# Keys with query weights, values with output weights: single loads of 39936-byte rows into four slots

## The chip, the cores and the metric

The kernel runs on one core of one Trainium2 chip. The metric is device time in microseconds (us), median of the runs shown; lower is better. A profile of one execution stands beside it, with times in us from the start of its span.

## The reference

One decode step of a transformer block, batch B=4, one token each, model width D=448, in float32. Attention has 16 query heads on 8 key/value heads of width 256 and looks at the last W=1024 of 4096 cached positions. Behind it stands an MLP with F=1792 hidden units. Cut to what is computed:

```python
def _A_ref(x, k_cache, v_cache, wq, wo):
    q = (x @ wq).reshape(B, 1, 16, 256).transpose(0, 2, 1, 3)
    k = repeat(k_cache[:, :, Sk - W:, :], 2, axis=1)
    v = repeat(v_cache[:, :, Sk - W:, :], 2, axis=1)
    p = softmax(einsum("bhqd,bhkd->bhqk", q, k) * 256 ** -0.5)
    o = einsum("bhqk,bhkd->bhqd", p, v)
    return o.transpose(0, 2, 1, 3).reshape(B, 1, 4096) @ wo

def _B_ref(x, w1, b1, w2, b2):
    return gelu(layernorm(x) @ w1 + b1) @ w2 + b2

h = x + _A_ref(layernorm(x), k_cache, v_cache, wq, wo)
out = h + _B_ref(layernorm(h), w1, b1, w2, b2)
```

Keys and values are 33.6 MB each, all weights together 21.1 MB; each byte is read once.

## The kernel before

The work goes by key/value head g = 0 to 7. `kernel` lays out all arrays on the host so that each load is a block of 128 rows, one for each partition, with its bytes contiguous. All large loads go through one ring of ten slots of 16 KB per partition (L37, L48), all are issued by the SP queue in program order, and each waits there until its slot is free.

For each head there are two loads of keys (`load_k`, L75, 2 MB, rows of 16384 bytes) and two of values (`load_v`, L79). `load_w` (L70) brings the query weights of head g+1 with the output weights of head g in rows of 14336 bytes. The order of the loads is: query weights 0, keys 0, weights, then for each g keys g+1, weights, values g. Head 7's values come in four loads of 1 MB. Then come the output weights of head 7 (wo7), w1 in two loads and w2 in three. The second load of w1 is completed by a small DMA from `w1e` (L53), whose outermost dimension is 8.

TensorE's order is that of the program (L275 to L305). In step g it does:

- `scores(g+1)` (L167): 32 matmuls s (L173), 16 for each half of the keys. VectorE takes the maximum (L177), ScalarE the exponentials (L184).
- `project_q(g+2)` (L152): matmuls pq and pqt.
- `values(g)` (L203): 32 matmuls po (L210) in four groups of eight, c = 0 to 3. After the second group stands `transpose_p(g+1)` (L193), passed in as `between`.
- `output(g)` (L229): VectorE scales po (L231), matmuls pot (L235) turn it, matmuls acc (L245) multiply with the output weights and add up over heads.

For g=7 there is no next head. acc is copied (L295) and folded into ph (L299), `output(7)` adds to ph (L251). `keep_warm` (L270) issues matmuls without use on an idle tile; in `values(7)` two follow each of the first three groups and three the last. Behind it stands the tail: h = x + attention (L336), its two layer norms, the hidden layer pu (L364), Gelu (L378), the transposes put (L383), the second layer py (L395), the sum (L399) and the output DMA (L400).

The four batch rows of a quantity sit on the first four partitions of each quarter of 32 partitions; the tail's matmuls after the first chunk use 4 columns of weights (`m`, L361 and L393). x, transposed, comes in a DMA of its own on the ScalarE queue (L57). x, b2 and b1 for the tail (`rs`) come in four DMAs of four rows (L128).

Of the kernel before, what the change touches and what calls it, by code (L numbers as in the profile page):

```python
# [8 lines left out]
F32 = mybir.dt.float32  # L9
# [18 lines left out]
E8 = 384  # L28
SLOT = 4096
EPS = 1e-5  # L30
SCALE = DH ** -0.5

@with_exitstack
def block_kernel(ctx: ExitStack, tc, x, rows, wq0, ww, kc, vc, wo7, w1, w1e, w2, out):
# [12 lines left out]

    def load(src, cols, name, eighths=0):  # L48
        t = ring.tile([P, SLOT], F32, tag="t", name=name)[:, :cols]
        n = cols - eighths  # L50
        nc.sync.dma_start(t[:, :n], src[:, :n])
        if eighths:
            nc.sync.dma_start(t[:, n:], w1e.rearrange("e (p c) -> e p c", c=E8)[:, :16, :])  # L53
        return t

    xT = const.tile([P, ND, B], F32, name="xT")
    nc.scalar.dma_start(xT, x.rearrange("p (a b) -> p a b", a=ND))  # L57


    def wq_parts(t):  # L60
        parts = [(a, a, slice(0, 512), t[:, a * 512 : (a + 1) * 512]) for a in range(3)]
        for i in range(2):
            parts.append((3, 3 + i, slice(i * 2 * P, (i + 1) * 2 * P), t[:, 3 * 512 :]))
        return parts

    def wo_rows(t):
        return t.rearrange("p (j e) -> p j e", j=4)


    def load_w(g):  # L70
        t = load(ww[g], 8 * D, f"ww{g}")
        return wq_parts(t[:, : 4 * D]), wo_rows(t[:, 4 * D :])


    def load_k(g):  # L75
        return [load(kc[g, i], 2 * B * 512, f"k{g}_{i}").rearrange("p (c b k) -> p c b k", c=2, b=B) for i in range(2)]


    def load_v(g):  # L79
        v, n = [], 2 if g == HKV - 1 else 4  # L80
        for c0 in range(0, NKC, n):
            t = load(vc[g, :, c0 * B * DH : (c0 + n) * B * DH], n * B * DH, f"v{g}_{c0}")
            t = t.rearrange("p (c b d) -> p c b d", c=n, b=B)
            v += [t[:, c : c + 2] for c in range(0, n, 2)]
        return v

# [26 lines left out]
    fold = fold.rearrange("p j q -> p (j q)")  # L113
    rows_of = ident.rearrange("p (j q) -> p j q", j=4)[:, :, :B]
    rows_of_pair = ident.rearrange("p (b q) -> p q b", b=B)
# [86 lines left out]

    def values(g, vt, between=None):  # L203
        if g == HKV - 1:
            tail.append(ps_t.tile([P, 2, 512], F32, tag="t", name="tail"))

        po = ps_o.tile([P, 2, DH], F32, tag="o", name=f"po{g}")
        for c in range(NKC // 2):
            for b in range(B):
                nc.tensor.matmul(  # L210
                    po[b * Q : (b + 1) * Q], pT[g % 2][:, c, b, :], vt[c][:, :, b, :],
                    start=(c == 0), stop=(c == NKC // 2 - 1),
                )
# [15 lines left out]
    def output(g, po, rec, wt):  # L229
        o = work.tile([P, 2, DH], F32, tag="o", name=f"o{g}")  # L230
        nc.vector.tensor_scalar_mul(o, po, rec)  # L231
# [10 lines left out]
        nc.vector.tensor_copy(dst[:, :, :, :B], pt)  # L242
# [12 lines left out]

    wqt = wq_parts(load(wq0, 4 * D, "wq0"))
    d = work.tile([P, ND, B], F32, tag="d", name="d_x")
# [7 lines left out]
    nc.vector.tensor_mul(yT[H:, 4, :B], d[H:, 3, :], rx[H:, :])  # L265
    project_q(0, wqt)

    tail = []

    def keep_warm(n):  # L270
        for _ in range(n):
            nc.tensor.matmul(tail[0][:Q, 0, :], idle[:, :Q], idle, start=True, stop=True)  # L272


    kt = load_k(0)  # L275
    wqt, wot = load_w(0)
    p, rec = scores(0, kt)
    project_q(1, wqt)
    transpose_p(0, p)
    for g in range(HKV):  # L280
        if g + 1 < HKV:
            kt = load_k(g + 1)
        if g + 2 < HKV:
            wqt, wo_next = load_w(g + 1)
        vt = load_v(g)
        if g + 1 == HKV:
            wot = wo_rows(load(wo7, 4 * D, "wo7"))
        if g + 1 < HKV:
            p, rec_next = scores(g + 1, kt)
        if g + 2 < HKV:  # L290
            project_q(g + 2, wqt)
        if g + 1 == HKV:

            accs = once.tile([P, D], F32, tag="u", name="accs")
            nc.scalar.copy(accs, acc)  # L295
            last = ps_s.tile([P, 2, 512], F32, tag="s", name="last")
            ph, pu = last[:, 1, :P].rearrange("p (i c) -> p i c", i=2), last[:, 0, :FQ]
            for j in range(4):
                nc.tensor.matmul(ph[j * Q : (j + 1) * Q], sel, columns(accs, j), start=True, stop=False)  # L299
        po = values(g, vt, (lambda: transpose_p(g + 1, p)) if g + 1 < HKV else None)  # L300
        output(g, po, rec, wot)
        if g + 1 < HKV:
            rec = rec_next
            if g + 2 < HKV:
                wot = wo_next  # L305

    w1t = []
    for a in (0, 2):
        n = 2 * F if a == 0 else F + F // 2
        t = load(w1[:, a * F : a * F + n], n, f"w1_{a}", eighths=E8 if a else 0)  # L310
        w1t += [t[:, :F], t[:, F:]]
    w2t = []
    for i, n in enumerate((8, 4, 2)):
        c0 = len(w2t)
        t = load(w2[:, c0 * D : (c0 + n) * D], n * D, f"w2_{i}").rearrange("p (c e) -> p c e", c=n)
        w2t += [t[:, c, :] for c in range(n)]

# [33 lines left out]
    nc.tensor.matmul(pz, z, rows_of, start=True, stop=True)  # L351
    nc.vector.tensor_copy(zT[:, :, :B], pz)
    hb = once.tile([P, P], F32, tag="hb", name="hb")
# [6 lines left out]
    for a in range(ND):  # L360
        m = Q if a == 0 else B  # L361
        for j in range(4):
            rows, w = w1_part(a, j)
            nc.tensor.matmul(  # L364
                pu[j * Q : j * Q + m, :], zT[rows, a, :m], w, start=(a == 0), stop=(a == ND - 1),
            )
# [19 lines left out]
    dst = gT[:, :12, :].rearrange("p (c j) q -> p c j q", c=3)  # L386
    nc.vector.tensor_copy(dst[:, :, :, :B], put[:, :3])
    for i, rows in enumerate((slice(0, H), slice(H, P))):
        nc.vector.tensor_copy(gT[rows, 12:, :B], put[rows, 3].rearrange("p (j i) q -> p j i q", i=2)[:, :, i, :])
    py = ps_o.tile([P, 2, H], F32, tag="o", name="py")  # L390
    for c in range(NFC):
        for j in range(4):
            m, n = (Q, 2) if c == 0 else (B, 2 if j < 3 else 1)  # L393
            w = columns(w2t[c], j) if n == 2 else w2t[c][:, None, 3 * P :]
            nc.tensor.matmul(  # L395
                py[j * Q : j * Q + m, :n, :], gT[:, c, :m], w, start=(c == 0), stop=(c == NFC - 1),
            )
    res = once.tile([P, P], F32, tag="res", name="res")
    nc.vector.tensor_add(res, py.rearrange("p i c -> p (i c)"), hb)  # L399
    nc.sync.dma_start(out, res)  # L400

# [62 lines left out]
```

## Time and profile before

| what | value |
|---|---|
| time, median of 3 runs | 217.79 us (217.52 to 217.93) |
| profiled execution, span | 215.9 us |
| instructions | 2546 |
| TensorE matmuls busy | 147.9 us, 69% |
| bytes read from HBM | 88.26 MB |
| mean granted TensorE clock | 0.842 |

The profile records one execution; its own time is known as the span from the first to the last instruction, 215.9 us, and the time of a run holds some 2 us more around it. Rows of a group read: line, engine, operation, tile written <- tiles read, shape, count | busy us, mean ns of one | idle time of the engine before them and what ended it. Rows of a stretch read: start:end, length, then busy us and count of TensorE matmuls, weight loads, VectorE, ScalarE and GpSimd, then granted clock, DMA share, GB/s. Rows of the timeline and of the chain begin with start and duration.

### The profile page before, as it was taken

The numbers are of one execution on the slowest core, as the hardware profiler recorded it, in microseconds if no ns is written. First come the engines' busy times: TensorE is split into PE (matmuls) and PEld (weight loads), VectorE is DVE, ScalarE is ACT, GpSimd is POOL, SyncE is SP. The second block draws the span as 40 slices with busy tenths as digits, with TensorE's granted clock in tenths as the row PEclk, the third lists the DMA queues.
The fourth block names the chain that finished last, engine by engine and source line by source line (L and its number), as shares of the span: only waits on it lengthen the run. The fifth ranks groups of instructions, "written<-read, shape, count | busy, mean of one in ns | idle before, by whom it ended". The sixth has DMA issues, their size and how long they took to land.

```text
span 215.9 us, 2546 instructions
## 1 busy us (share of the span) xinstructions
PE 147.9 (69%) x1077; PEld 61.0 (28%) x1077; DVE 35.7 (17%) x138; ACT 20.7 (10%) x49; POOL 5.6 (3%) x17
## 2 busy tenths in 40 slices
PE   0478854578469764776568845876477838789994
PEld 0341413131143303231142304231142203235443
DVE  1411311011110111021200131011201020201230
ACT  0210303000210003000210003000300011000310
POOL 6100000000000000000000000000000000000110
PEclk9999998596967888596958787696959796969999
DMA  6999999999999999999999999999999999999991
GB/s 250 422 425 427 428 432 430 420 428 429 427 431 422 431 421 432 425 431 422 431 428 425 429 425 433 428 425 424 435 419 431 434 423 410 419 427 418 350 396 49
DMA packets 7379, 88.49 MB, mean 410 GB/s; under 512 B 952, under 2 KB 1208, under 8 KB 1736
## 3 DMA queue, kind: packets, MB, share of 16 engines
q1 hardware_dynamic: 7192, 88.28, 97.2%
q8 instruction: 8, 0.13, 0.2%
q10 hardware_dynamic: 176, 0.05, 0.1%
q14 instruction: 3, 0.02, 0.0%
HBM read 88.26 MB, written 0.07 MB: 409 GB/s over the span
## 4 chain that ended last, share of the span: by engine, by line
DMA 72%; PE 22%; issue 2%; DVE 2%; ACT 1%; SPq 0%
DMA v<-vc 53%; DMA k<-kc 16%; PE po L210 6%; PE s L173 2%; DMA xT<-x 2%; PE tail L272 2%; PE py L395 2%; PE last L364 2%; PE pot L235 1%; PE pq L155 1%; PE pqt L161 1%; DVE o L231 1%; PE acc L245 1%; ACT qs L157 1%; PE last L251 0%
## 5 line engine op out<-in xcount | busy, mean ns | idle before, releaser
L210 PE MATMUL po<-v,pT 128*32 128x512 f32 x256 | 44.3, 805 | 12.8 <-DMA v<-vc 12.8
L173 PE MATMUL s<-k,qT 128*32 128x512 f32 x256 | 40.4, 761 | 13.6 <-DMA k<-kc 12.4
L184 ACT ACTIVATE p<-s,nm 128x512 f32<-128x512 f32 x16 | 10.8, 683 | 134.6 <-DVE nm L180 134.6
L173 PEld LDWEIGHTS s<-k,qT 128*32 128x32 f32 x256 | 8.5, 124 | 42.2 <-DVE mx L177 22.8
L177 DVE TENSOR_REDUCE mx<-s 128x1 f32<-128x512 f32 x16 | 11.1, 692 | 53.2 <-PE s L173 53.2
L161 PE MATMUL pqt<-sel,qs 128*128 128x4 f32 x64 | 13.9, 340 | 6.0 <-ACT qs L157 6.0
L155 PE MATMUL pq<-ww,yT 128*32 128x512 f32 (+1 forms) x70 | 7.5, 513 | 14.2 <-DMA ww<-ww 14.2
L210 PEld LDWEIGHTS po<-v,pT 128*32 128x32 f32 x256 | 8.8, 130 | 29.1 <-issue 20.4
L161 PEld LDWEIGHTS pqt<-sel,qs 128*128 128x128 f32 x64 | 13.2, 306 | 10.2 <-ACT qs L157 10.2
L235 PE MATMUL pot<-ident,o 128*128 128x8 f32 x64 | 8.5, 259 | 6.4 <-DVE o L231 6.4
L235 PEld LDWEIGHTS pot<-ident,o 128*128 128x128 f32 x64 | 7.7, 191 | 13.2 <-DVE o L231 13.2
L196 PEld LDWEIGHTS ppt<-ident,p 128*128 128x128 f32 x64 | 7.6, 152 | 11.2 <-issue 11.2
L231 DVE TENSOR_SCALAR o<-po,rec 128x512 f32<-128x512 f32 x8 | 6.0, 751 | 22.1 <-PE po L210 22.1
L196 PE MATMUL ppt<-ident,p 128*128 128x128 f32 x64 | 9.4, 294 | 0.0
L155 PEld LDWEIGHTS pq<-ww,yT 128*32 128x32 f32 x70 | 2.9, 108 | 21.6 <-issue 20.1
L200 DVE COPY pT<-ppt 128x32 f32<-128x32 f32 x16 | 2.3, 187 | 38.7 <-PE ppt L196 38.7
L245 PE MATMUL acc<-ww,oT 128*32 128x448 f32 x56 | 6.7, 551 | 1.9 <-DVE oT L242 1.9
L272 PE MATMUL tail<-idle 128*32 128x512 bf16 x25 | 7.5, 402 | 0.0
L157 ACT COPY qs<-pq 128x512 f32<-128x512 f32 x8 | 4.7, 585 | 21.2 <-PE pq L155 21.2
L149 POOL TENSOR_TENSOR r<-ve_r,mhalf 128x1 f32<-128x1 f32 x2 | 1.1, 542 | 195.2 <-DVE ve_r L148 195.2
L165 DVE COPY qT<-pqt 128x16 f32<-128x16 f32 x16 | 2.1, 170 | 23.8 <-PE pqt L161 23.8
L134 PE MATMUL pm_x<-xT,mean 128*128 128x12 f32 x2 | 0.6, 362 | 5.8 <-DMA xT<-x 5.8
(93 smaller groups left out, 55.9 us busy)
## 6 DMA issues: line engine op xcount, KB each, us to landing
k<-kc SPq DMA_DIRECT2D x16, 2048.0 KB, 34.9
v<-vc SPq DMA_DIRECT2D x14, 2048.0 KB, 37.7
ww<-ww SPq DMA_DIRECT2D x7, 1792.0 KB, 18.4
v<-vc SPq DMA_DIRECT2D x4, 1024.0 KB, 36.1
w<-w SPq DMA_DIRECT2D x2, 1792.0 KB, 24.2
w<-w SPq DMA_DIRECT2D x1, 1152.0 KB, 24.8
wq<-wq SPq DMA_DIRECT2D x1, 896.0 KB, 4.7
wo<-wo SPq DMA_DIRECT2D x1, 896.0 KB
```

The costliest lines, as they stand in the source:

```text
L155: nc.tensor.matmul(pq[j * Q : (j + 1) * Q, cols], yT[:, a, :], w, start=True, stop=True)
L157: nc.scalar.copy(qs, pq)
L161: nc.tensor.matmul(pt[:, i, :], qs[:, i * P : (i + 1) * P], sel[:, :B], start=True, stop=True)
L173: nc.tensor.matmul(s[b * Q : (b + 1) * Q, h, :], qT[g % 2][:, c, b, :], kt[h][:, c, b, :], start=(c == 0), stop=(c == 1),)
L177: nc.vector.reduce_max(mx[:, h : h + 1], s[:, h, :], axis=AX.X)
L184: nc.scalar.activation(p[:, h * 512 : (h + 1) * 512], s[:, h, :], AF.Exp, bias=nm, scale=SCALE, accum_out=sums[:, h : h + 1],)
L196: nc.tensor.transpose(pt[:, c, :], p[:, c * P : (c + 1) * P], ident)
L210: nc.tensor.matmul(po[b * Q : (b + 1) * Q], pT[g % 2][:, c, b, :], vt[c][:, :, b, :], start=(c == 0), stop=(c == NKC // 2 - 1),)
L231: nc.vector.tensor_scalar_mul(o, po, rec)
L235: nc.tensor.matmul(pt[:, c], o[:, i, c * P : (c + 1) * P], rows_of_pair[:, i * REP : (i + 1) * REP, :], start=(i == 0), stop=(i == 1),)
L245: nc.tensor.matmul(acc[i * Q : (i + 1) * Q, :], oT[g % 2][:, i, :], wt[:, i, :], start=(g == 0), stop=(g == HKV - 2),)
L272: nc.tensor.matmul(tail[0][:Q, 0, :], idle[:, :Q], idle, start=True, stop=True)
```

## The change

Ring and slots: four slots of 39936 bytes per partition instead of ten of 16384. A head's keys and the next head's query weights become one array `kw` with rows of 39936 bytes, a head's values and output weights one array `vw`; each is one load. Head 7 has no next query weights and loads 32768 bytes of its row. Head 7's values come in two DMAs into one slot, three quarters and one quarter. wo7 and w1 share a slot (three DMAs), w2 has one (three DMAs of 8, 4 and 2 chunks). `w1e` is gone. The first query weights and the transposed x come as one load (`first`).

`transpose_p(g+1)` moves from the middle of `values(g)` to ahead of it. In `values(7)` only the last group is followed by keep-warm matmuls. The batch rows sit on every eighth partition, so that x and the biases (`rows`, 16 rows) come in one DMA, the output is 16 rows instead of 128, and the tail's matmuls use all 32 columns.

```diff
-E8 = 384
-SLOT = 4096
+GAP = Q // B
+KV = 8 * B * DH
+WC = 4 * D
+SLOT = KV + WC
+V7A = 6 * B * DH
+W1C = 3 * F + F // 2
...
-    ring = ctx.enter_context(tc.tile_pool(name="ring", bufs=10))
+    ring = ctx.enter_context(tc.tile_pool(name="ring", bufs=4))
...
+    t0 = const.tile([P, WC + X0], F32, name="first")
+    nc.sync.dma_start(t0, first)
...
     def load_k(g):
-        return [load(kc[g, i], 2 * B * 512, f"k{g}_{i}").rearrange("p (c b k) -> p c b k", c=2, b=B) for i in range(2)]
+        t = load(kw[g] if g < HKV - 1 else kw[g][:, :KV], f"k{g}")
+        k = t[:, :KV].rearrange("p (h c b k) -> p h c b k", h=2, c=2, b=B)
+        return [k[:, h] for h in range(2)], wq_parts(t[:, KV:]) if g < HKV - 1 else None
...
     def load_v(g):
+        t = load(vw[g], f"v{g}")
+        return chunk_pairs(t[:, :KV]), wo_rows(t[:, KV:])
+
+    def load_v7():
+        t = slot("v7")
+        for a, b in ((0, V7A), (V7A, KV)):
+            nc.sync.dma_start(t[:, a:b], v7[:, a:b])
+        return chunk_pairs(t[:, :KV])
...
-    for j in range(4):
-        nc.scalar.dma_start(rs[j * Q : j * Q + B, :], rows[j])
+    nc.scalar.dma_start(rs[::GAP, :], rows)
+    def spread(t):
+        return t[..., ::GAP]
...
-            if c == 1 and between is not None:
-                between()
-            if g == HKV - 1:
-                keep_warm(2 if c < NKC // 2 - 1 else 3)
+            if g == HKV - 1 and c == NKC // 2 - 1:
+                keep_warm(3)
...
         if g + 1 < HKV:
-            kt = load_k(g + 1)
...
+            kt, wqt = load_k(g + 1)
+            vt, wot = load_v(g)
             p, rec_next = scores(g + 1, kt)
-        if g + 2 < HKV:
-            project_q(g + 2, wqt)
+            if g + 2 < HKV:
+                project_q(g + 2, wqt)
+            transpose_p(g + 1, p)
+        else:
+            vt = load_v7()
+            tw = slot("w1")
+            wot = wo_rows(tw[:, :WC])
+            nc.sync.dma_start(tw[:, :WC], wo7)
+            tw1 = tw[:, WC : WC + W1C]
+            for a, n in ((0, 2 * F), (2 * F, W1C - 2 * F)):
+                nc.sync.dma_start(tw1[:, a : a + n], w1[:, a : a + n])
+            tw2 = slot("w2")
+            for c0, n in ((0, 8), (8, 4), (12, 2)):
+                nc.sync.dma_start(tw2[:, c0 * D : (c0 + n) * D], w2[:, c0 * D : (c0 + n) * D])
...
-            m, n = (Q, 2) if c == 0 else (B, 2 if j < 3 else 1)
+            n = 2 if c == 0 or j < 3 else 1
...
-                py[j * Q : j * Q + m, :n, :], gT[:, c, :m], w, start=(c == 0), stop=(c == NFC - 1),
+                py[j * Q : (j + 1) * Q, :n, :], gT[:, c, :], w, start=(c == 0), stop=(c == NFC - 1),
...
-    nc.sync.dma_start(out, res)
+    nc.sync.dma_start(out, res[::GAP, :])
```

More of the change, by code (lines that the diff above doesn't have):

```diff
@@ L27 @@
 Q = 32
-E8 = 384
-SLOT = 4096
+GAP = Q // B
+KV = 8 * B * DH
+WC = 4 * D
+SLOT = KV + WC
+X0 = 64
+V7A = 6 * B * DH
+W1C = 3 * F + F // 2
 EPS = 1e-5
@@ L33, in block_kernel @@
 @with_exitstack
-def block_kernel(ctx: ExitStack, tc, x, rows, wq0, ww, kc, vc, wo7, w1, w1e, w2, out):
+def block_kernel(ctx: ExitStack, tc, rows, first, kw, vw, v7, wo7, w1, w2, out):
     nc = tc.nc
     const = ctx.enter_context(tc.tile_pool(name="const", bufs=1))
-    ring = ctx.enter_context(tc.tile_pool(name="ring", bufs=10))
+    ring = ctx.enter_context(tc.tile_pool(name="ring", bufs=4))
     work = ctx.enter_context(tc.tile_pool(name="work", bufs=2))
@@ L44, in block_kernel, with slot, load @@
     ps_w = ctx.enter_context(tc.tile_pool(name="ps_w", bufs=1, space=PSUM))
[L48 to L53, printed above, removed]
-        return t
-    xT = const.tile([P, ND, B], F32, name="xT")
-    nc.scalar.dma_start(xT, x.rearrange("p (a b) -> p a b", a=ND))
+    def slot(name):
+        return ring.tile([P, SLOT], F32, tag="t", name=name)
+    def load(src, name):
+        n = src.shape[-1]
+        t = slot(name)[:, :n]
+        nc.sync.dma_start(t, src)
+        return t
+    t0 = const.tile([P, WC + X0], F32, name="first")
+    nc.sync.dma_start(t0, first)
+    xT = t0[:, WC : WC + ND * B].rearrange("p (a b) -> p a b", a=ND)
     def wq_parts(t):
@@ L62, in wq_parts @@
         for i in range(2):
-            parts.append((3, 3 + i, slice(i * 2 * P, (i + 1) * 2 * P), t[:, 3 * 512 :]))
+            parts.append((3, 3 + i, slice(i * 2 * P, (i + 1) * 2 * P), t[:, 3 * 512 : 4 * D]))
         return parts
@@ L67, in wo_rows, with chunk_pairs @@
         return t.rearrange("p (j e) -> p j e", j=4)
-    def load_w(g):
-        t = load(ww[g], 8 * D, f"ww{g}")
-        return wq_parts(t[:, : 4 * D]), wo_rows(t[:, 4 * D :])
     def load_k(g):
-        return [load(kc[g, i], 2 * B * 512, f"k{g}_{i}").rearrange("p (c b k) -> p c b k", c=2, b=B) for i in range(2)]
-    def load_v(g):
[L80 to L85, printed above, removed]
+        t = load(kw[g] if g < HKV - 1 else kw[g][:, :KV], f"k{g}")
+        k = t[:, :KV].rearrange("p (h c b k) -> p h c b k", h=2, c=2, b=B)
+        return [k[:, h] for h in range(2)], wq_parts(t[:, KV:]) if g < HKV - 1 else None
+    def chunk_pairs(t):
+        t = t.rearrange("p (c b d) -> p c b d", c=NKC, b=B)
+        return [t[:, c : c + 2] for c in range(0, NKC, 2)]
+    def load_v(g):
+        t = load(vw[g], f"v{g}")
[5 more added lines that the diff above has]
+        return chunk_pairs(t[:, :KV])
     ident = const.tile([P, P], F32, name="ident")
@@ L113, in block_kernel @@
     fold = fold.rearrange("p j q -> p (j q)")
-    rows_of = ident.rearrange("p (j q) -> p j q", j=4)[:, :, :B]
+    rows_of = ident.rearrange("p (j b e) -> p j b e", j=4, b=B)[:, :, :, 0]
     rows_of_pair = ident.rearrange("p (b q) -> p q b", b=B)
@@ L200, in transpose_p, with values @@
             nc.vector.tensor_copy(pT[g % 2][:, :, :, i * REP : (i + 1) * REP], src[:, :, i, :, :REP])
-    def values(g, vt, between=None):
+    def values(g, vt):
         if g == HKV - 1:
@@ L241, in output @@
         dst = oT[g % 2].rearrange("p (r c) q -> p c r q", r=REP)
-        nc.vector.tensor_copy(dst[:, :, :, :B], pt)
+        nc.vector.tensor_copy(spread(dst), pt)
         for i in range(4):
@@ L254, in output @@
                 )
-    wqt = wq_parts(load(wq0, 4 * D, "wq0"))
     d = work.tile([P, ND, B], F32, tag="d", name="d_x")
@@ L265, in block_kernel @@
     nc.vector.tensor_mul(yT[H:, 4, :B], d[H:, 3, :], rx[H:, :])
-    project_q(0, wqt)
+    project_q(0, wq_parts(t0[:, :WC]))
     tail = []
@@ L299, in block_kernel @@
                 nc.tensor.matmul(ph[j * Q : (j + 1) * Q], sel, columns(accs, j), start=True, stop=False)
-        po = values(g, vt, (lambda: transpose_p(g + 1, p)) if g + 1 < HKV else None)
+        po = values(g, vt)
         output(g, po, rec, wot)
@@ L303, in block_kernel @@
             rec = rec_next
[L304 to L316, printed above, removed]
+    w1t = [tw1[:, a * F : (a + 1) * F] for a in range(3)] + [tw1[:, 3 * F :]]
+    w2t = [tw2[:, c * D : (c + 1) * D] for c in range(NFC)]
     def w1_part(a, j):
@@ L351, in block_kernel @@
     nc.tensor.matmul(pz, z, rows_of, start=True, stop=True)
-    nc.vector.tensor_copy(zT[:, :, :B], pz)
+    nc.vector.tensor_copy(spread(zT), pz)
     hb = once.tile([P, P], F32, tag="hb", name="hb")
@@ L360, in block_kernel @@
     for a in range(ND):
-        m = Q if a == 0 else B
         for j in range(4):
@@ L364, in block_kernel @@
             nc.tensor.matmul(
-                pu[j * Q : j * Q + m, :], zT[rows, a, :m], w, start=(a == 0), stop=(a == ND - 1),
+                pu[j * Q : (j + 1) * Q, :], zT[rows, a, :], w, start=(a == 0), stop=(a == ND - 1),
             )
@@ L386, in block_kernel @@
     dst = gT[:, :12, :].rearrange("p (c j) q -> p c j q", c=3)
-    nc.vector.tensor_copy(dst[:, :, :, :B], put[:, :3])
+    nc.vector.tensor_copy(spread(dst), put[:, :3])
     for i, rows in enumerate((slice(0, H), slice(H, P))):
-        nc.vector.tensor_copy(gT[rows, 12:, :B], put[rows, 3].rearrange("p (j i) q -> p j i q", i=2)[:, :, i, :])
+        nc.vector.tensor_copy(spread(gT[rows, 12:, :]), put[rows, 3].rearrange("p (j i) q -> p j i q", i=2)[:, :, i, :])
     py = ps_o.tile([P, 2, H], F32, tag="o", name="py")
@@ L429 @@
     wo = np.asarray(A_wo).reshape(HKV, 4, P, D).transpose(0, 2, 1, 3).reshape(HKV, P, 4 * D)
-    ww = np.concatenate([wq[1:], wo[:-1]], axis=2)
+    first = np.concatenate([wq[0], xT, np.zeros((P, X0 - ND * B), np.float32)], axis=1)
+    kw = np.concatenate([k, np.concatenate([wq[1:], np.zeros((1, P, WC), np.float32)])], axis=2)
+    vw = np.concatenate([v[:-1], wo[:-1]], axis=2)
     w1 = packed(np.asarray(B_w1))
-    w1e = np.concatenate([w1[:, -E8:].reshape(8, 16 * E8), np.zeros((8, E8), np.float32)], axis=1)
     w2 = np.asarray(B_w2).reshape(4, FQ, D)
@@ L447 @@
     rows = np.concatenate([quadrants(xp), quadrants(b2), quadrants(np.asarray(B_b1).reshape(1, F))], axis=2)
+    rows = rows.reshape(4 * B, -1)
     arrays = {
-        "x": xT, "rows": rows, "wq0": wq[0], "ww": ww, "kc": k, "vc": v, "wo7": wo[-1], "w1": w1, "w1e": w1e, "w2": w2,
+        "rows": rows, "first": first, "kw": kw, "vw": vw, "v7": v[-1], "wo7": wo[-1], "w1": w1, "w2": w2,
     }
@@ L456 @@
     ]
-    out = nc.dram_tensor("out", (P, P), F32, kind="ExternalOutput").ap()
+    out = nc.dram_tensor("out", (4 * B, P), F32, kind="ExternalOutput").ap()
     with tile.TileContext(nc) as tc:
@@ L461 @@
     r = run(nc, [arrays], core_ids=[0])
-    got = np.asarray(r.results[0]["out"]).reshape(4, Q, P)[:, :B, :]
+    got = np.asarray(r.results[0]["out"]).reshape(4, B, P)
     return np.ascontiguousarray(got.transpose(1, 0, 2).reshape(B, 1, 4 * P)[:, :, :D])
```

14 lines of the change are left out of this document (3 added, 11 removed).

## The prediction

> **What bounds the kernel now.** I read the first page from the top: busy shares, the slices, the queues.
>
> ```profile
> span 215.9 us, 2546 instructions
> PE 147.9 (69%) x1077; PEld 61.0 (28%) x1077; DVE 35.7 (17%) x138; ACT 20.7 (10%) x49; POOL 5.6 (3%) x17
> DMA  6999999999999999999999999999999999999991
> GB/s 250 422 425 427 428 432 430 420 428 429 427 431 422 431 421 432 425 431 422 431 428 425 429 425 433 428 425 424 435 419 431 434 423 410 419 427 418 350 396 49
> q1 hardware_dynamic: 7192, 88.28, 97.2%
> HBM read 88.26 MB, written 0.07 MB: 409 GB/s over the span
> ```
>
> No compute engine is near its limit, while the DMA engines are busy in every slice but the first and last. All of it is one queue, and its 88.28 MB don't change. So the first question is what rate the engines give, the second what happens after the stream. The chain that ended last, from the landing of the last piece of v6 (g=6), shows the second (columns: start, us, what):
>
> ```profile
> 183.87 0.04 issue
> 183.91 1.97 PE po L210 x16
> 185.91 0.76 DVE o L231
> 189.65 0.42 PE last L299 x8
> 190.07 1.49 PE po L210 x8
> 195.40 1.14 PE po L210 x5
> 196.57 0.76 DVE o L231
> 199.84 0.65 PE tail L272 x3
> 209.56 2.82 PE py L395 x62
> 212.38 0.09 issue
> 212.47 0.66 PE py L395 x4
> 213.16 0.29 DVE res L399
> ```
>
> From 183.87 on there is no DMA piece: TensorE works through the second half of values(6), output(6), values(7), output(7) and the MLP without a break. Yet the stream isn't slack: py stops for 0.09 us at 212.38, just before its last two chunks, and these are what the last load brings. By stages:
>
> ```profile
> 202.00:206.00 4.00, 4.00 (x33) 1.44 (x32) 0.77 (x4) 1.69 (x3) 0.60 (x2) 1.00 1.02 351
> 210.00:214.00 4.00, 3.00 (x104) 2.37 (x94) 0.29 (x1) 0.00 (x0) 0.00 (x0) 1.00 0.23 89
> ```
>
> (The last three columns are granted clock, DMA share, GB/s.) A share of 0.23 of the last 4 us puts the end of the stream near 211; with its landing that is the stop at 212.38. **Two chains end together**: the stream, and TensorE's work counted from the landing of v6. A gain in the stream alone is worth nothing unless TensorE gains as well, and TensorE gains only by an earlier landing of v6 or by less work behind it.
>
> **The change, the stream.** Rows get longer, their bytes stay. What a row costs beside its bytes, the rates show:
>
> ```profile
> 60.00:90.00 30.00, 20.74 (x130) 8.73 (x130) 3.75 (x14) 2.62 (x6) 0.00 (x0) 0.74 1.01 427
> 64.00:76.00 12.00, 10.57 (x72) 3.66 (x72) 1.22 (x4) 0.00 (x0) 0.00 (x0) 0.78 1.00 426
> 150.00:180.00 30.00, 19.30 (x131) 7.11 (x135) 4.82 (x17) 3.48 (x9) 0.00 (x0) 0.83 1.01 428
> 184.00:191.00 7.00, 5.21 (x48) 1.98 (x49) 0.93 (x2) 0.53 (x1) 0.00 (x0) 0.94 1.01 421
> rs<-rows ACTq DMA_DIRECT2D x4, 11.0 KB
> out<-res SPq DMA_DIRECT2D x1, 64.0 KB
> ```
>
> The 30-us stretches move rows of 16384 B (and 14336 B), 426 to 428 GB/s, middle 427; the stretch 184 to 191 moves v7's 8192-byte rows at 421. On 16 engines a 16384-byte row takes 16 x 16384 / 427 = 613.9 ns, an 8192-byte one 16 x 8192 / 421 = 311.3 ns. Two of the short less one of the long is **8.8 ns per row**; with 426 and 422 it is 5.8, with 428 and 420 11.7. No row of 39936 B is in the trace; at the same price it takes 1475 + 9 ns, or 431 GB/s. Nothing excludes that so long a row is slower; that is a rival below.
>
> Ahead of v6's end the kernel loads 38 times 128 rows (wq0, 16 of k, 14 of v, 7 of ww), afterwards 16 times (first, 8 of k, 7 of v). That is 22 x 128 / 16 = 176 rows fewer per engine: 176 x 8.8 ns = 1.55 us (1.0 to 2.1). To the end of the stream it is 24 loads instead of 48, and w1e's 128 rows go too: 200 rows, 1.75 us. The biases came in four DMAs of 4 rows (11.0 KB each); if these sit on 4 of 16 engines, those carry 4 x 2816 B / 26.7 B per ns = 0.4 us more than the others, and every later load lands with them; 16 rows in one DMA spread to 0.1 us each. Between 0 and 0.3 us earlier; I take 0.3. The stretch at 351 GB/s, where w1_2 and w1e are due, may be w1e's doing and would then go; it lies behind v6 and only moves the end of the stream. So **v6 lands 1.85 us earlier, at 182.0**, and the stream ends about 2.05 us earlier.
>
> Does the stream still run without a break with four slots? A load waits for the slot of the load four before it. A 39936-byte load takes 5.11 MB / 427 = 12.0 us, so three loads behind cover 36 us from landing to release. TensorE is busy 147.9 us over some 17 loads, under 9 us each, and even doubled by its waits that is 18. The SP queue, which issues all of them in order, has nothing else to issue; half of the cover is left. x now lands with wq0 as one load of 0.95 MB, in place of 0.9 MB beside it; the first scores then wait for k0 whole, some 1 us later than now, covered by the 12 us until k1 lands. I cost both at nothing.
>
> **The change, TensorE behind v6.** Now v6 comes in two loads, and half of values(6) is done before 183.87. Afterwards it lands whole, and all 32 matmuls stand behind it. Their price depends on the granted clock:
>
> ```profile
> 135.54 3.60 PE L210 MATMUL po<-v,pT 128*32 128x512 f32 x16 [1.09 <-DMA v<-vc]
> 140.45 1.92 PE L210 MATMUL po<-v,pT 128*32 128x512 f32 x16 [0.28 <-DMA v<-vc]
> 179.09 2.88 PE L210 MATMUL po<-v,pT 128*32 128x512 f32 x16 [2.97 <-DMA v<-vc]
> 176.51:179.92 3.41, 0.83 (x8) 0.34 (x12) 1.00 (x5) 1.45 (x4) 0.00 (x0) 1.00 1.01 425
> 179.92:183.34 3.42, 3.42 (x19) 1.72 (x12) 0.00 (x0) 0.00 (x0) 0.00 (x0) 0.50 0.96 402
> 186.75:190.16 3.41, 2.49 (x28) 1.46 (x32) 0.17 (x1) 0.53 (x1) 0.00 (x0) 1.00 1.02 423
> 190.16:193.58 3.42, 3.42 (x18) 0.88 (x11) 0.00 (x0) 0.00 (x0) 0.00 (x0) 0.50 1.03 429
> 197.00:213.20 16.20, 15.39 (x221) 8.79 (x220) 3.96 (x19) 2.77 (x7) 1.08 (x2) 1.00 0.86 330
> ```
>
> Sixteen take 3.6 us at half clock, 1.95 at full. A stretch of 3.4 us with little work (176.51, with the wait of 2.97) is followed by one at half clock, a busy one by full clock. Afterwards k7 lands at 182.0 - 12.0 = 170.0, and TensorE has 32 score matmuls, 3.9 to 7.2 us; then it waits for the softmax:
>
> ```profile
> L184 ACT ACTIVATE p<-s,nm 128x512 f32<-128x512 f32 x16 | 10.8, 683 | 134.6 <-DVE nm L180 134.6
> L177 DVE TENSOR_REDUCE mx<-s 128x1 f32<-128x512 f32 x16 | 11.1, 692 | 53.2 <-PE s L173 53.2
> ```
>
> That is 0.7 + 2 x 0.7 us, and the transposes, which now stand ahead of values, are too small to count as a burst. So for 4 to 8 us before 182.0 there is almost no matmul work, and values(6) starts at half clock, with between 1.5 and 5 us of it left, since full clock comes only after a stretch of 3.4 us that was busy. With 3.2 us: 14 matmuls in it, 18 in 2.2 us, **5.4 us** (3.9 all full, 7.2 all half); values(6) ends at 187.4.
>
> From its end to the start of values(7) nothing changes: 185.88 to 190.07, 4.2 us. So values(7) starts at 191.6; its first three quarters have landed (182.0 + 7.4), the last lands at 191.8 and is needed 3 us later. Today values(7) takes 190.07 to 196.54, 6.5 us, with six keep-warm matmuls inside it that are removed: at 0.22 us (0.65 for three) at full clock and twice that at half, two and four of them, 1.7 us. That leaves 4.8 with the half-clock stretch lying just on its start, the dearest place; 3.9 without it, 5.5 with all of it. I take 4.6, near the row. It ends at **196.2**, against 196.54: of 1.85 us of earlier landing, 0.3 are left, since 3.4 us of matmuls have come behind the landing and only 1.9 went.
>
> The skill speaks against the change here. The Trainium skill, "TensorE: Matmul & The Clock Gate", section "HAM oscillation — how this bites in real kernels", says that a wait longer than its activity window of about 3.4 us halves the clock for the next burst; the stretches above agree (0.5 behind 2.97 us of waiting). The same page, section "What's actually happening", says that this window runs free of the kernel's start, so that its placement cannot be known beforehand; one trace can't show that.
>
> **The change, the rest.** The MLP's matmuls load 32 columns instead of 4, and the transposed copies write every eighth column:
>
> ```profile
> L395 PE MATMUL py<-w,gT 128*4 128x128 f32 x78 | 3.2, 272 | 0.1
> L395 PE MATMUL py<-w,gT 128*32 128x128 f32 x8 | 0.4, 281 | 0.4 <-DVE gT L387 0.4
> ```
>
> 281 against 272 ns for overlapping matmuls: nothing, at worst 9 ns x 28 in a row of one quarter, 0.25 us. The stop of 0.1 us before the last chunks goes, as the stream ends 2 us earlier. The output shrinks from 128 rows of 512 B to 16, seven fewer on each engine: 7 x (19 + 9 ns) = 0.2 us. **Sum: -0.3 - 0.1 - 0.2 = -0.6 us**, a span of 215.3. The profile gives the span alone; the median of the runs is 1.9 us above it (217.52 to 217.93), which I keep: 217.2.
>
> **The rivals.**
> (1) TensorE meets full clock in both bursts: 182.0 + 3.9 + 4.2 + 3.9 = 194.0, 2.5 earlier; then the stream's end decides, 2.05 + 0.2 earlier: 215.5. Against it speaks the idle time before v6.
> (2) Slower: the half clock falls on both bursts, since a whole load leaves TensorE waiting longer in one piece and the keep-warm matmuls are gone. Up to 182.0 + 7.2 + 4.2 + 5.5 = 198.9, 2.4 later less 0.3; with 6.5 and 5.2, near 218.9. It decides once the two bursts take over 10.9 us together (I took 10.0). That is what the page's rule gives when its window falls badly.
> (3) The long rows don't run faster, so that the change does not do what it is built for: v6 at 183.9, then 5.4 + 4.2 + 4.6 ends at 198.1, 1.5 later less 0.2: 219.1. The 8.8 ns speak against it, for it that it rests on 6 GB/s.
> (4) Waits by slot, not by piece: wo7 shares a slot with w1, whose end lands at 182.0 + 8.3 MB / 427 = 201.5, and output(7) would wait for it some 3 us: 220. Against it:
>
> ```profile
> 207.67 0.69 ACT L378 ACTIVATE u<-u 128x256 f32<-128x256 f32 x2 [3.89 <-DVE u L377]
> 208.14 0.84 PE L383 MATMUL put<-ident,u 128*128 128x16 f32 x6
> ```
>
> TensorE reads the first half of u at 208.14 while ScalarE writes the second until 208.36: pieces are waited for one by one.
>
> **How the numbers follow.** My case 0.46 (own range 216.5 to 217.8), (1) 0.15, (2) 0.20, (3) 0.12, (4) 0.04, others 0.03. Within 0.2%, 217.35 to 218.23, is about what a measurement cannot tell from no change: 0.10 of my case, 0.07 of (2) and the others' 0.03 lie there. Faster: 0.36 + 0.15 = 0.51; same 0.20; slower 0.13 + 0.12 + 0.04 = 0.29. The range 215.5 to 219.0 takes in (1), my case, most of (2) and half of (3).
>
> **What would show it.** The stretches of 30 us at 430 to 432 GB/s; at 427 or less (3) holds. The first matmul of values(6) near 182.0 and 32 of them in 5 to 6 us behind it; the clock row of that stretch at 0.5 or a mix. No DMA stop before py's end. values(7) without a wait for its last quarter. What would make me wrong: TensorE waiting for w1 at output(7), a load issued only after the queue ran dry, or another clock in the 16 us after values(7), which I left at 1.00.

## The result, and the profile after

| | before | after |
|---|---|---|
| median of 20 runs each, us | 217.71 | 217.55 |
| ratio, 95% interval | | 0.9994 (0.9971 to 1.0017) |
| profiled execution, span, us | 215.9 | 217.3 |
| instructions | 2546 | 2466 |

No change that can be measured. The forecast was 217.2 us with the likeliest case "a little faster". One thing the medians hide: nineteen of the twenty runs of before lie within 217.5 to 217.9 us, while the changed kernel's go from 216.6 to 220.65. The ratios, here and below, leave out runs over 1.5% above the fastest of the same kernel: of the changed kernel the five from 220.45 to 220.65 us, of swap two at 223.2. With those five its mean is 218.4 us against 217.8, 0.3% longer; none of them was profiled. The profiled execution took 219.05 us; eleven of the twenty are shorter. Its page begins:

```profile
span 217.3 us, 2466 instructions
PE 151.9 (70%) x1071; PEld 57.4 (26%) x1071; DVE 35.7 (16%) x138; ACT 20.2 (9%) x49; POOL 5.6 (3%) x17
DMA  7999999999999999999999999999999999999930
GB/s 293 435 397 471 426 397 466 426 399 463 434 415 441 426 426 441 444 404 449 434 426 429 441 434 419 441 422 426 456 401 451 405 459 404 393 425 417 420 120 5
q1 hardware_dynamic: 3488, 88.25, 94.9%
```

3488 packets instead of 7192, for the same bytes. The last two slices hold 120 and 5 GB/s, where before they held 396 and 49: the stream ends earlier, although the span is longer. The stretches (granted clock, DMA share, GB/s in the last columns) give the rate, and the stretch from 202, which stood at 351:

```profile
60.00:90.00 30.00, 21.03 (x144) 8.22 (x140) 5.35 (x21) 3.87 (x10) 0.00 (x0) 0.75 0.99 427
90.00:120.00 30.00, 23.57 (x138) 7.03 (x138) 3.49 (x12) 1.94 (x5) 0.00 (x0) 0.68 1.01 432
120.00:150.00 30.00, 18.71 (x130) 6.79 (x130) 4.42 (x14) 1.94 (x5) 0.00 (x0) 0.78 1.00 431
150.00:180.00 30.00, 21.67 (x144) 6.97 (x137) 5.38 (x18) 3.38 (x9) 0.00 (x0) 0.77 0.99 427
202.00:206.00 4.00, 4.00 (x29) 1.56 (x28) 0.99 (x5) 2.09 (x5) 0.38 (x1) 1.00 1.00 420
206.00:210.00 4.00, 4.00 (x32) 1.56 (x28) 1.40 (x5) 0.69 (x2) 0.71 (x2) 1.00 0.50 202
```

Two of the four 30-us stretches reach the 431 to 432 GB/s of the forecast, two stand at 427 as before. From 30 to 180 us the changed kernel averages 430 GB/s and the kernel before 427 (the rows stand under short).

And the chain behind the landing of v6:

```profile
182.48 0.14 issue
182.62 6.21 PE po L219 x32
191.00 1.63 PE acc L252 x8
193.23 0.66 PE last L310 x8
193.89 3.90 PE po L219 x32
197.81 0.76 DVE o L238
210.91 3.30 PE py L395 x66
214.23 0.29 DVE res L399
```

v6 lands at 182.48 instead of 183.87, and py runs through without a stop at its last chunks: the stream no longer decides. But values(6) now takes 6.21 us behind the landing instead of 1.97, and what follows up to values(7) takes 5.06 us (188.83 to 193.89) instead of 4.19. values(7) takes 3.90 instead of 6.47. The sum of those, -1.3 + 4.2 + 0.9 - 2.6, is 1.2 us at the end of values(7). From there to the start of res the chain is 0.2 us shorter (16.44 us, before 16.62), and from res to the end of the span 0.3 us longer, at the output's store. That makes the 1.4 us between the spans.

### The profile page after: what moved, and what is told of

The parts are those of the page before. It is cut to its first block, busy times and chain, and to the rows that moved or that the text cites. A ratio compares the mean times of both kernels' runs of the same rounds, so it can differ in the third digit from the quotient of the medians.

```text
span 217.3 us, 2466 instructions
## 1 busy us (share of the span) xinstructions
PE 151.9 (70%) x1071; PEld 57.4 (26%) x1071; DVE 35.7 (16%) x138; ACT 20.2 (9%) x49; POOL 5.6 (3%) x17
## 3 DMA queue, kind: packets, MB, share of 16 engines
q1 hardware_dynamic: 3488, 88.25, 94.9%
## 4 chain that ended last, share of the span: by engine, by line
DMA 70%; PE 25%; DVE 2%; issue 1%; SPq 1%; ACT 0%
DMA v<-vw 70%; PE po L219 13%; PE acc L252 3%; PE pot L242 2%; PE tail L278 2%; DVE o L238 2%; PE last L364 2%; PE py L395 2%; PE last L258 0%; SPq L59 0%; DVE oT L249 0%; PE put L383 0%; PE last L310 0%; PE tail L328 0%; PE pm L328 0%
## 5 line engine op out<-in xcount | busy, mean ns | idle before, releaser
L182 PE MATMUL s<-k,qT 128*32 128x512 f32 x256 | 46.3, 860 | 24.0 <-DMA k<-kw 17.5
L182 PEld LDWEIGHTS s<-k,qT 128*32 128x32 f32 x256 | 8.4, 136 | 60.4 <-DMA k<-kw 20.6
L186 DVE TENSOR_REDUCE mx<-s 128x1 f32<-128x512 f32 x16 | 11.1, 692 | 73.0 <-PE s L182 73.0
L219 PEld LDWEIGHTS po<-v,pT 128*32 128x32 f32 x256 | 10.6, 151 | 39.4 <-issue 32.8
L170 PE MATMUL pqt<-sel,qs 128*128 128x4 f32 x64 | 9.3, 268 | 6.1 <-ACT qs L166 6.1
L170 PEld LDWEIGHTS pqt<-sel,qs 128*128 128x128 f32 x64 | 8.6, 208 | 10.7 <-ACT qs L166 10.7
L252 PE MATMUL acc<-v,oT 128*32 128x448 f32 x56 | 9.6, 764 | 2.0 <-DVE oT L249 2.0
L164 PE MATMUL pq<-k,yT 128*32 128x512 f32 (+1 forms) x70 | 8.1, 554 | 0.0
L164 PEld LDWEIGHTS pq<-k,yT 128*32 128x32 f32 x70 | 3.7, 124 | 7.4 <-issue 6.1
L278 PE MATMUL tail<-idle 128*32 128x512 bf16 x19 | 5.3, 382 | 0.0
L143 PE MATMUL pm_x<-first,mean 128*128 128x12 f32 x2 | 0.6, 363 | 5.5 <-DMA first<-first 5.5
L164 PE MATMUL pq<-first,yT 128*32 128x512 f32 (+1 forms) x10 | 1.9, 885 | 2.9 <-DVE yT L270 2.9
```

What stands on the lines that cost most here:

```text
L164: nc.tensor.matmul(pq[j * Q : (j + 1) * Q, cols], yT[:, a, :], w, start=True, stop=True)
L170: nc.tensor.matmul(pt[:, i, :], qs[:, i * P : (i + 1) * P], sel[:, :B], start=True, stop=True)
L182: nc.tensor.matmul(s[b * Q : (b + 1) * Q, h, :], qT[g % 2][:, c, b, :], kt[h][:, c, b, :], start=(c == 0), stop=(c == 1),)
L186: nc.vector.reduce_max(mx[:, h : h + 1], s[:, h, :], axis=AX.X)
L219: nc.tensor.matmul(po[b * Q : (b + 1) * Q], pT[g % 2][:, c, b, :], vt[c][:, :, b, :], start=(c == 0), stop=(c == NKC // 2 - 1),)
L252: nc.tensor.matmul(acc[i * Q : (i + 1) * Q, :], oT[g % 2][:, i, :], wt[:, i, :], start=(g == 0), stop=(g == HKV - 2),)
```

## The experiments

**Theory A**: the stream did get shorter, TensorE's work behind the landing of v6 eats the gain, and how much of it depends on where stretches of half clock fall, which differs in each execution. **Theory B**: the long loads themselves vary, and spread and loss come from the stream. **Theory C** concerns w1e: that it evened the engines, so that its removal costs something.

Ratios are to runs of the kernel before on the same chip, timed in turn with these (medians 217.9 to 218.0 us). Medians are of all runs of a kernel; again is a single run.

| run | what | median, us | ratio (95%) |
|---|---|---|---|
| again | after, unaltered | 217.25 | one run |
| halves | after, v6 in two loads | 216.82 | 0.9946 (0.9922 to 0.9970) |
| warm | after, idle matmuls behind head 7's scores | 215.44 | 0.9895 (0.9870 to 0.9920) |
| short | after, rows of 13312 bytes | 219.19 | 1.0040 (1.0015 to 1.0065) |
| swap | before, all of values(6) behind the landing | 222.03 | 1.0132 (1.0092 to 1.0172) |
| no_w1e | before without w1e | 217.41 | 0.9985 (0.9966 to 1.0005) |
| warm_out | warm, output of 128 rows | 215.18 | 0.9881 (0.9863 to 0.9899) |
| warm_w1e | warm with w1e | 216.76 | 0.9940 (0.9928 to 0.9952) |
| short_warm | no_w1e with idle matmuls | 216.96 | 0.9959 (0.9946 to 0.9971) |
| best | warm_out, halves, shorter last load | 215.60 | 0.9892 (0.9877 to 0.9907) |
| best2 | best, idle matmuls moved ahead | 215.45 | 0.9878 (0.9861 to 0.9894) |

**again** has no edit.

> The changed kernel once more, unaltered, for a second profile. Theory A (the granted clock of the bursts values(6) and values(7) sets the time, and its 3.4 us stretches lie elsewhere in each execution): v6 lands within 0.3 us of 182.5 again, while values(6), its wait for output(6) and values(7) together differ by over 0.5 us from the 15.2 us of the first profile, and the clock rows of the two bursts differ; the span differs by the same amount. Theory B (the stream varies between executions): the bursts take the same 15.2 us and the landing of v6 moves with the span.

Its span is 215.5 us, 1.8 less than the first profile's. Its chain:

```profile
182.55 0.14 issue
182.69 5.61 PE po L219 x32
190.47 1.00 PE acc L252 x8
192.08 0.43 PE last L310 x8
192.51 3.48 PE po L219 x32
```

v6 lands 0.07 us from where it landed in the first profile; the bursts and what lies between them take 13.3 us instead of 15.2, and that is the difference of the spans. The clock of these stretches, first profile ahead:

```profile
180.93:187.76 6.83, 5.14 (x28) 1.39 (x31) 0.00 (x0) 0.00 (x0) 0.00 (x0) 0.50 0.95 407
187.76:191.17 3.41, 2.26 (x24) 1.24 (x20) 0.94 (x2) 0.00 (x0) 0.00 (x0) 1.00 0.96 401
191.17:194.58 3.41, 2.78 (x24) 0.66 (x20) 0.00 (x0) 0.53 (x1) 0.00 (x0) 0.50 1.07 447
```

```profile
179.81:186.63 6.82, 4.07 (x22) 1.12 (x24) 0.29 (x2) 0.00 (x0) 0.00 (x0) 0.50 1.02 435
186.63:190.05 3.42, 2.55 (x24) 1.19 (x16) 0.75 (x1) 0.00 (x0) 0.00 (x0) 1.00 0.90 378
190.05:193.46 3.41, 2.48 (x30) 0.84 (x33) 0.19 (x1) 0.53 (x1) 0.00 (x0) 1.00 1.01 421
```

The same kernel at the same landing: in the first profile the grid of 3.41-us steps lies 1.1 us later, half clock holds 1.1 us longer into values(6), and a second half-clock step falls on the multiplication with the output weights (1.63 us instead of 1.00). Theory A; B would have moved the landing.

**halves**, in `load_v`:

```diff
-        t = load(vw[g], f"v{g}")
+        t = slot(f"v{g}")
+        cuts = (0, KV // 2, SLOT) if g == HKV - 2 else (0, SLOT)
+        for n0, n1 in zip(cuts, cuts[1:]):
+            nc.sync.dma_start(t[:, n0:n1], vw[g][:, n0:n1])
```

> The changed kernel with v6 loaded in two DMAs, half the keys' positions first, so that 16 of the 32 matmuls of values(6) run before the rest lands, as before the change. Theory A: only 16 matmuls, 2.0 to 3.6 us, stand behind the landing at 182.5 instead of 3.9 to 6.2; the time falls by 1.5 to 2.6 us, to 215.2 to 216.2 us, with a spread under 1.5 us. Theory B, or the stream's end deciding: no change, 217.5 us with the same spread.

Faster than before by 0.5%, and so by 1.0 us than after (0.9946 against 0.9994), where 1.5 to 2.6 were expected; single runs from 215.4 to 217.9, a spread not under 1.5. In the profile, of its shortest run (215.43), values(6) is over before v7 is there:

```profile
180.24 5.34 PE L222 MATMUL po<-v,pT 128*32 128x512 f32 x32
189.97 3.64 PE L222 MATMUL po<-v,pT 128*32 128x512 f32 x32 [0.15 <-DMA v<-v]
```

So less work behind the landing helps, as A has it, but doesn't make the kernel independent of the clock.

**warm** puts idle matmuls into values(6)'s own PSUM tile, which its first real matmul starts anew (`idle_on`), and keeps some behind it; loads are untouched:

```diff
             p, rec_next = scores(g + 1, kt)
...
+            po = new_po(g) if g == HKV - 2 else None
+            if po is not None:
+                idle_on(po, 6)
             transpose_p(g + 1, p)
+            if po is not None:
+                idle_on(po, 8)
...
-            if g == HKV - 1 and c == NKC // 2 - 1:
+            if g >= HKV - 2 and c == NKC // 2 - 1:
                 keep_warm(3)
...
-        if g == HKV - 1:
+        if g >= HKV - 2:
             keep_warm(2)
...
             vt = load_v7()
+            keep_warm(3)
```

> The changed kernel with 14 idle matmuls while TensorE waits for the softmax of head 7 and for v6, and 8 more between values(6) and values(7); loads untouched. Theory A: both bursts run at full clock, 3.9 us each, values(7) ends near 194.8 instead of 197.8, and the time is 215.3 to 216.3 us in every execution, spread under 1 us. Theory B: no change, 217.5 us with 3 us of spread, since the idle matmuls touch neither the stream nor its order.

215.44 us, near the lower end of what A gave and 2.1 us from what B gave. Four of six runs lie between 215.29 and 215.45, two at 216.5 and 216.6, which A had not foreseen: the spread is 1.3 us where A had under 1. The chain and the clock:

```profile
182.55 0.04 issue
182.59 3.69 PE po L226 x32
190.55 3.48 PE po L226 x32
210.54 0.29 DVE res L413
```

```profile
181.29:184.70 3.41, 3.16 (x25) 0.97 (x27) 0.00 (x0) 0.00 (x0) 0.00 (x0) 1.00 0.99 425
184.70:188.12 3.42, 3.17 (x28) 1.55 (x21) 0.75 (x1) 0.00 (x0) 0.00 (x0) 1.00 0.94 402
188.12:191.53 3.41, 3.38 (x34) 1.22 (x37) 0.19 (x1) 0.53 (x1) 0.00 (x0) 1.00 0.98 409
```

The landing stays at 182.55; both bursts run at full clock. Work that computes nothing takes 2.2 us off (0.9895 against 0.9994).

**short** undoes the long rows alone:

```diff
-        nc.sync.dma_start(t, src)
+        step = SLOT // 3 if n == SLOT else n
+        for n0 in range(0, n, step):
+            nc.sync.dma_start(t[:, n0 : n0 + step], src[:, n0 : n0 + step])
```

> The changed kernel with each 39936-byte load cut into three DMAs of 13312-byte rows into the same slot; all else untouched. If the length of the rows made the stream faster, at 8.8 ns per row: 224 rows more per engine ahead of v6's end, v6 lands 2.0 us later, near 184.5, stretches of 30 us at 426 GB/s instead of 431, and the time rises by 2 us, to about 219.5. If the stream gained by the other parts (w1e gone, biases in one DMA): v6 lands at 182.5 as in the changed kernel, and the time stays.

1.0 us slower than after by the ratios (1.0040 against 0.9994), where 2 were expected for a later landing alone. With all runs counted it is only 0.2 us (ratios of the means 1.0039 against 1.0028), so the time shows the price of the rows badly. The landing shows it better. That of v6 can't be read, since values(6) follows the late transposes at 184.29 without a wait; that of k7 can, in after's timeline and then in short's:

```profile
170.70 3.59 PE L182 MATMUL s<-k,qT 128*32 128x512 f32 x16 [2.55 <-DMA k<-kw]
```

```profile
172.85 3.64 PE L184 MATMUL s<-k,qT 128*32 128x512 f32 x16 [3.66 <-DMA k<-kw]
```

2.15 us later, with 13 loads ahead of it that have two pieces more each: 13 x 2 x 128 / 16 = 208 rows per engine, **10.3 ns per row**, where 8.8 was taken from the rates of before. In five other profiles with the long rows these matmuls, waiting for k7, start between 170.63 and 170.84, so 2.15 us is no scatter. The rate from 30 to 180 us, in before, after and short, goes the same way:

```profile
30.00:180.00 150.00, 101.51 (x661) 38.40 (x665) 22.29 (x77) 13.63 (x34) 0.00 (x0) 0.79 1.01 427
30.00:180.00 150.00, 107.62 (x674) 35.89 (x666) 22.82 (x78) 13.07 (x34) 0.00 (x0) 0.73 1.00 430
30.00:180.00 150.00, 106.73 (x648) 39.23 (x638) 20.92 (x72) 11.62 (x30) 0.00 (x0) 0.83 1.01 426
```

**swap** starts from the kernel before and takes over from the change, at head 6 alone, that all of values(6) stands behind the last landing, with the transposes ahead of it:

```diff
-        for c0 in range(0, NKC, n):
+        for c0 in range(0, NKC, n) if g != HKV - 2 else (4, 0):
...
+        if g == HKV - 2:
+            v = v[2:] + v[:2]
...
-        po = values(g, vt, (lambda: transpose_p(g + 1, p)) if g + 1 < HKV else None)
+        if g + 2 == HKV:
+            transpose_p(g + 1, p)
+        po = values(g, vt, (lambda: transpose_p(g + 1, p)) if g + 2 < HKV else None)
```

> The kernel before with two edits at head 6 alone: its two loads of values come in the other order, so that the half that values(6) begins with lands last, and the transposes of head 7 stand ahead of values(6). So all 32 matmuls stand behind the last landing, near 183.9, as in the changed kernel, with the short rows and the ten slots kept. Theory A (work behind the landing of v6 eats what the stream gains): 2 to 4 us more behind the landing, 219.5 to 221.5 us, with a spread of 2 to 3 us instead of 0.4. Theory B (the changed kernel's spread and loss come from its long loads or slots): no change, 217.8 us, spread under 0.6.

1.3% slower, 2.9 us, with compared runs from 219.6 to 222.1 and two more at 223.2. So the loss and the spread come with short rows and ten slots too; Theory B falls.

**no_w1e** loads w1's second part whole: `t = load(w1[:, a * F : a * F + n], n, f"w1_{a}")`.

> The kernel before, w1's second load as one DMA of 128 rows, without w1e. Theory A (w1e slows the stretch from 202 to 206, 351 GB/s): that stretch rises above 410, the stream ends up to 0.7 us earlier, and the time falls by at most 0.2 us, since TensorE's chain ends at the same moment. Theory C (w1e loads half of the engines, the ones that are ahead, and so evens their ends): the stretch rises too, but the last engine ends up to 0.5 us later, and the time rises by 0.3 to 0.5 us.

C expected it slower, and it is not: 217.41, -0.15% with an interval that reaches zero, which fits A. Single runs go from 216.9 to 219.3 where before has 217.8 to 218.3; its profile, of one of the longest (219.15), has no stop before py's last chunks, so there TensorE decides. The stream is over by 211.0 us, in before by 212.0. This suggests, without a run of its own, that the end of the stream kept the times of before together: with that end earlier, TensorE's spread shows. The stretch that held 351 GB/s:

```profile
202.00:206.00 4.00, 4.00 (x28) 1.85 (x30) 1.12 (x6) 2.09 (x5) 0.04 (x1) 1.00 1.01 429
```

**warm_w1e** puts w1e into warm:

```diff
-            for a, n in ((0, 2 * F), (2 * F, W1C - 2 * F)):
+            for a, n in ((0, 2 * F), (2 * F, W1C - 2 * F - E8)):
                 nc.sync.dma_start(tw1[:, a : a + n], w1[:, a : a + n])
+            nc.sync.dma_start(tw1[:, W1C - E8 :], w1e.rearrange("e (p c) -> e p c", c=E8)[:, :16, :])
```

> The changed kernel with the idle matmuls of the run warm and, as before the change, the last 384 columns of w1 in the small DMA w1e of outermost dimension 8. With warm the stream and TensorE end together (py ends at 210.5, the last load is there at 209.7). If w1e evens the engines: the stream ends 0.5 to 0.8 us earlier, the time falls by at most 0.1 us, as TensorE then decides. If w1e only slows the stream: it ends up to 0.7 us later, py stops before its last chunks, 215.4 to 216.0 us.

1.3 us slower than warm, more than either reading gave, and the chain now ends on the stream:

```profile
190.06 20.88 DMA w<-w
211.08 0.68 PE py L411 x4
```

py waits for the last load until 211.08. C falls: on this stream w1e only costs time. Whether that is its outermost dimension or its 128 rows of 1536 bytes, these runs do not separate.

**warm_out** stores all 128 rows of `res` again and picks the 16 on the host's side of the output.

> The changed kernel with the idle matmuls of the run warm, and the output stored as 128 rows, as before the change, instead of 16 spread ones. If the store of 16 spread rows is the dearer one (0.55 us of issue and 2.7 us to the end of the span, against 0.35 and 2.4 before): 0.25 us less than warm, 215.2 us. If the fewer rows are the cheaper ones: 0.2 us more, 215.65.

215.18, 0.26 less, as expected from the two profiles (issue 0.55 us against 0.35 before): the store of fewer, spread rows is the dearer one. The intervals of the two ratios overlap, but four of five runs (215.07 to 215.20) lie under all of warm's; the fifth is 216.41.

**short_warm** is no_w1e with ten idle matmuls ahead of values(6) and those of warm behind it; the six between the groups of values(7) are gone.

> The kernel before without w1e and with idle matmuls ahead of values(6) and between values(6) and values(7), those inside values(7) taken out: short rows and ten slots, TensorE held at full clock behind v6. It gives what short rows can reach, beside 215.4 of the run warm. If the long rows are worth the 1.5 us that the count of rows gives: 216.7 to 217.1 us, stream's end the limit, with a small spread. If w1e and TensorE's clock were the whole of the gain: 215.4 to 215.8 us.

216.96, all runs within 0.2 us, the last load deciding. With TensorE held at full clock on both sides, 39936-byte rows and what comes with them are worth 216.96 - 215.44 = 1.5 us, or 1.8 against warm_out, which stores the same 128 rows. In warm TensorE, not the stream, ends last, so the stream alone may have gained more.

**best** adds halves to warm_out and makes w2's loads 8, 5 and 1 chunks.

> The changed kernel with the idle matmuls of warm, the output stored as 128 rows, v6 in two loads, and w2's last load one chunk instead of two. TensorE's chain then ends some 2 us before the stream's; the stream decides, with 8 instead of 16 matmuls behind its last landing: 214.9 to 215.2 us in every execution. If TensorE still decides: 215.2 as with the output alone.

A miss: 215.60. Its profile is that of its longest run (216.6 us):

```profile
175.17 3.64 PE L185 MATMUL s<-k,qT 128*32 128x512 f32 x16 [0.81 <-DVE mx L189]
182.15 1.68 PE L220 MATMUL po<-idle 128*32 128x512 bf16 x7
183.89 3.60 PE L229 MATMUL po<-v,pT 128*32 128x512 f32 x29
```

scores(7) ran at half clock to its end, the transposes came late, and the eight idle matmuls behind them stood in front of values(6), whose first half had landed long before (best2, with the same loads up to there, computes on it from 178.85).

**best2** moves them and makes w2's loads 8, 4 and 2 chunks again:

```diff
+            if po is not None:
+                idle_on(po, 6)
             p, rec_next = scores(g + 1, kt)
...
             transpose_p(g + 1, p)
-            if po is not None:
-                idle_on(po, 8)
```

> As the run best, with w2's last load two chunks again, and the idle matmuls moved: six ahead of scores(7) instead of eight behind the transposes of head 7, so that none stands in front of values(6), whose first half can begin when it has landed. If the slower runs of warm and best (216.4 to 216.6) come from scores(7) at half clock, with the idle matmuls behind it holding up values(6): 215.0 to 215.3 us in every execution, the stream's end deciding. If they have another cause: the same median with single runs over 216.3.

All five runs between 215.30 and 215.53, none near 216.5; the median is 0.15 above the upper end expected. Of the 16 runs of warm, warm_out and best, four lie at 216.4 to 216.6, so five without one are a hint and no proof. TensorE now waits for the stream three times, at the second half of v6, at v7 and before py's last chunks:

```profile
182.76 1.92 PE L229 MATMUL po<-v,pT 128*32 128x512 f32 x16 [1.99 <-DMA v<-vw]
190.17 3.64 PE L229 MATMUL po<-v,pT 128*32 128x512 f32 x32 [1.17 <-DMA v<-v]
```

```profile
206.97 2.95 PE py L412 x63
209.92 0.07 issue
210.00 0.68 PE py L412 x4
```

The stream sets the time, by the landing of v7 and by its end. A short stop costs more than its length: py takes 3.70 us with this one of 0.07, and 3.37 in warm, where it runs through. best2 is 1.2% faster than before, as warm_out is, and in these few runs the steadier of the two.

## Why the prediction was right, and where not

- **Two chains that end together.** Right. The stream ends over 2 us earlier and the time didn't move; with TensorE held at full clock the same stream gives 215.44 (warm).
- **The price of a row.** 8.8 ns was low by a little: 10.3 by short. The long rows run at 427 to 432 GB/s, 430 on average, where 431 was worked out. Two stretches at 427 were the sign named for rival (3); the average and short speak against it.
- **v6 lands 1.85 us earlier.** 1.39 (182.48) and 1.32 (182.55) against the one profile of before. In two other profiles with the short rows, no_w1e and short_warm, the matmuls that wait for it start at 184.23 and 184.22, 0.3 later than in before (183.91); against them the gain is 1.6 to 1.7, near the 1.55 for the rows. No run shows the term of 0.3 us for the biases in one DMA.
- **Four slots don't break the stream.** Right; the DMA row is 9 from the second slice to the end of the stream.
- **values(6) whole behind the landing, at half clock first.** Right in kind; 5.4 us was too little: 6.21 and 5.61.
- **"From its end to the start of values(7) nothing changes", 4.2 us.** This step failed in the first profile (5.06) and held in the second (4.21). It took the clock of one execution for that of the kernel; a half-clock step on acc and last costs 0.9 us.
- **values(7), 4.6 us.** 3.90 and 3.48: too much. The half-clock step was put on its start. In the first profile that step began earlier, at 191.17, and left 0.7 us for values(7); in the second there was none there.
- **What makes a step of half clock.** A busy stretch was to be followed by full clock. One with 2.49 us of matmuls in 3.41 was followed by half clock (186.75 in before), one with 2.55 in 3.42 by full clock (186.63 in again), so how busy it must be does not follow from these rows. And the wait of 2.97 us in the stretch from 176.51, set beside the 3.4 us of the window, is shorter than it.
- **The tail, -0.1 for the stop before py's last chunks.** Too little: py takes 3.30 us instead of 3.57, though its matmuls load 32 columns. The tail up to res gains 0.2 in all.
- **The output, -0.2.** Wrong in sign: +0.26 (warm_out). The count of rows was no measure of this store.
- **w1e.** The suspicion that the 351 GB/s stretch was its doing is confirmed by no_w1e and warm_w1e.
- **The sum.** -0.6 against -0.2 for the medians, inside the range. That the number came so near is in part luck: a later landing, a longer values(6) and a dearer store were set off by a shorter values(7). In the second profile the span comes out at 215.5 by this, where 215.3 was forecast; in the first it is 217.3. The changed kernel's runs lie in three groups, 216.6 to 217.6, 219.05 to 219.6 and 220.45 to 220.65; the upper two, nine runs of twenty, are above the range that was given for the median. My case and rival (2) are the same kernel in different executions, but rival (2) had the half clock on both bursts, and in the first profile it fell on values(6) and on acc and last. A single number with a chance for each was the wrong form; it is a spread by the placement of the clock's steps, from one run to the next. Rivals (3) and (4) fell: the rows are faster, and output(7) never waited for w1.

What the Trainium skill says on this ("TensorE: Matmul & The Clock Gate", section "What's actually happening": the activity window runs free of the kernel's start) could not be seen in one trace. The two profiles of the changed kernel, whose steps lie 1.1 us apart against the same landing, agree with it.

Not settled: what makes the changed kernel's five runs above 220.4 us, and what makes warm's two runs of 216.5 and 216.6 and warm_out's of 216.41. That these three are best's case is likely from best's profile and from best2, where none was seen in five runs, but no profile of them was taken.

## What to carry to other kernels

Where a stream is the limit, the end of the kernel hangs on the last landing that compute still has to follow: larger loads speed the stream by a price per row (10 ns here) and put a whole load's compute behind that landing; cut only the last loads small. If compute behind a landing comes after a wait, count the first part of it at half clock (values(6) took 5.6 to 6.2 us here, 3.7 when TensorE was kept busy ahead of it), and fill the wait with idle matmuls that do not stand in front of the data. If a kernel's runs suddenly spread, ask whether its limit has changed, even if the median hasn't moved: here the runs went from 0.4 us apart (all but one) to 4.0.

## What the runs showed that I had not expected

- A small DMA with an outermost dimension of 8, 0.2 MB, cost 1.3 us at the end of the stream (warm_w1e against warm).
- With both halves of the keys landing at once, the second half of the scores waits 0.8 us for VectorE's maximum of the first (8 times in after, once before): `PE s L182 <- DVE mx L186: 6.5, 8, 0.8` (us in all, times, longest).
- Storing 16 spread rows took 0.26 us longer than storing 128 (warm against warm_out).
